# Identity products in place of transposes for step 0, masks on the tensor engine for three steps, three attention units to a bank, and 512-column transposes of x

## The chip, the cores and the metric

The kernel runs on one core of a Trainium2 chip. Times are device microseconds (us) of an execution; a kernel's time is the median over its runs. PE is the tensor engine (PEld its weight loads), DVE the vector engine, ACT the scalar engine, POOL the GpSimd engine, SP the sync engine. POOL and SP here only issue transfers (DMAs), apart from a few constants that POOL makes at the start.

## What is computed

Sliding-window attention with sink keys, and on its result a feed-forward layer with a rational activation:

```python
batch, n_heads, seq, head_dim = 4, 8, 768, 64
n_sink, window = 4, 128
scores = q @ k.T / sqrt(head_dim)
keep = (key < n_sink) | ((0 <= query - key) & (query - key < window))
a = softmax(where(keep, scores, -1e9))
x = (a @ v) laid out as (3072 tokens, 512)
h = x @ w_in                                  # 512 x 2048
P = a[0] + a[1]*h + a[2]*h**2 + a[3]*h**3
Q = 1 + abs(b[0])*abs(h) + abs(b[1])*h**2
out = (P / (Q + 1e-6)) @ w_out                # 2048 x 512
```

Inputs and the output are fp32; the products run in bf16 and accumulate in fp32.

## The kernel before

**Steps.** The 3072 tokens are cut into 12 steps of 256 (three to a batch entry). A step s has an attention part and then a feed-forward part, called m there.

*Attention.* Heads go in pairs, i = 0 to 3; two pairs make a group. k of a step is transposed and spread over `kT_fix` so that 64 keys of both heads of a pair fill one 128x128 weight (`spread_k`, L333 to L344). `scores` (L382) makes four products of 64 keys by 192 queries for a pair, into one tile of two PSUM banks; `exps` (L395, ACT) takes the exponential into `e_fix`; `mask` (L404, DVE) multiplies the two 64-column edge blocks of every 64 keys of a group by 0 and 1. Sink keys have products and exponentials of their own (L356, L366, and for the first step of a batch entry a small mask, L374). `attend` (L412) multiplies the exponentials of a pair with v, to which a column of ones is added for the softmax's sum: two tiles of 128 queries, 130 columns each, in one bank. `normalize` (L435) takes the reciprocal of the sums and multiplies, writing 256 columns of `x_n`. So a step has four attends and four normalizations, all on the bank `ps_m`, and each attend waits until the normalization before it has emptied that bank (in step 0 every second one uses `ps_o`). x is then transposed into `xblk`: in steps 0 to 2 on PE (`turn_x`, copied by ACT in `place_x`), from step 3 on by SP's transposing DMAs, four to a step, each 128 rows by 256 columns (`turn_x_tile`, L465).

*Feed-forward.* `project_in` (L475) makes 64 products of 256 columns in four blocks (called gemm1 in the plan), into the two-bank tiles `ps_h`, of which there are two; ACT copies each block into `hb`. DVE and ACT compute the activation in halves or whole tiles of 4096 columns: squares, |h|, denominator, polynomial, and 1/Q as exp(-ln Q) on ACT; `gate` is the last multiplication. The square of the first half is on ACT (step 0: DVE), that of the second half on DVE (L504; last step: ACT). `project_out` (L555) makes 2 x 16 products of 512 columns into `ps_o` (in the last four steps one of two into `ps_m`), ACT copies the result, SP stores it.

**The start.** q and k of step 0 come in by SP as fp32 (q as three tokens to a partition, k as two, so that the DMA has long runs), are cast by ACT (`cast_q3`) and DVE (`cast_k2`), transposed by PE, and put into order of tokens as they leave PSUM: `place_q3` (L275, ACT) writes bf16 with a stride of three, `spread_k2` (L312, DVE) with a stride of two, in eight copies. All other k, q, v and the weights come through POOL's cast DMAs. Those of steps 1 and 2 (`turn_k2`, `turn_q1`) are transposed by PE, later ones by SP's DMAs (L291, L307).

**Who sets the order.** The whole program is a list of pieces (`piece`, L586), each with its engine, an assumed length, a rank (a due time; four units are a step), the pieces it comes after, and the PSUM tile that it takes or frees. `run_list` (L842) plays these lengths forward: whenever an engine is free it takes the able piece of the lowest rank. The order that comes out is fixed in the program; each engine runs its list strictly in that order and waits where a piece's inputs are late on the chip. Where the plan leaves PE idle, `spin` (L351) is put in: products of the identity with itself that no one reads. POOL's and SP's DMAs are planned with an assumed load each, and at most eight of each kind are in flight.

## Time and profile before

| what | value |
|---|---|
| median of 11 runs | 276.99 us (273.23 to 280.5) |
| time of the profiled execution | 274.26 us |
| its span, first to last instruction | 272.5 us |
| PE busy, instructions | 245.9 us (90%), 2230 |
| DVE busy | 237.7 us (87%), 324 |
| ACT busy | 222.5 us (82%), 215 |
| POOL busy | 122.2 us (45%), 178 |
| software DMA queue (POOL) | 74288 packets, 12.99 MB, 77.5% of 16 engines' span |
| hardware DMA queue (SP) | 35936 packets, 14.73 MB, 28.4% |
| mean granted PE clock | 0.987 |

Busy time counts an instruction from its start to its end; a matmul's end is modelled, and neighbours overlap, so a PE that shows busy also holds the filler products of L353 (27.8 us in 334). Idle time in a row of a group is time that the engine stood just before it, with what ended the wait. In the chain of waits, which is followed back from the last instruction, each row is what the next one waited for. All engines run their lists in order, so a wait also holds up what stands behind it.

### The profile page before, as it was taken

To read this page: it belongs to the slowest core of one execution; us is meant where nothing else is said; L and a number is where in the kernel's file an instruction comes from. 1 tells how busy PE (TensorE), PEld (TensorE's weight loads), DVE (VectorE), ACT (ScalarE), POOL (GpSimd) and SP (SyncE) were. 2 spreads that over 40 slices of the span, in tenths; PEclk is the share of its full clock that TensorE was granted. 3 is DMA by queue.
4 is the path that set the end of the run, shared out by engine and by line. 5 is a ranking of instruction groups with operands and counts; after the bars stand their busy time and mean duration, and the time that the engine had idled before them with its cause. 6 is when DMAs were issued, how large, how long until landed. Compare 5 with 4: busy or idle time off the path is not lost.

```text
span 272.5 us, 5564 instructions
## 1 busy us (share of the span) xinstructions
PE 245.9 (90%) x2230; PEld 183.2 (67%) x2230; DVE 237.7 (87%) x324; ACT 222.5 (82%) x215; POOL 122.2 (45%) x178
## 2 busy tenths in 40 slices
PE   5768987998993799998999999998999999999895
PEld 5656976876861687786767757776676867665443
DVE  7774668999981899999999999999999999899960
ACT  8831787859996668999898989979989899799931
POOL 8945799789885776492951331560000000000000
PEclk9997999999999799999999999999999999999999
DMA  6999999999999999999999543381011111010132
GB/s 192 98 157 192 58 108 164 133 139 162 156 115 146 159 187 182 162 112 116 139 168 53 106 61 67 44 76 58 19 45 56 44 66 51 19 53 26 38 115 77
DMA packets 110249, 28.06 MB, mean 103 GB/s; under 512 B 102032, under 2 KB 106128, under 8 KB 110224
## 3 DMA queue, kind: packets, MB, share of 16 engines
q0 software_dynamic: 74288, 12.99, 77.5%
q1 hardware_dynamic: 35936, 14.73, 28.4%
q8 instruction: 17, 0.28, 0.4%
q14 instruction: 8, 0.07, 0.1%
HBM read 27.30 MB, written 6.29 MB: 123 GB/s over the span
## 4 chain that ended last, share of the span: by engine, by line
DVE 39%; DMA 15%; PE 14%; issue 11%; POOL 11%; ACT 9%; DVEq 0%; POOLq 0%
DVE den L515 6%; DVE sq L531 6%; PE ps_out L563 5%; DVE x_n L444 4%; PE ps_h L480 4%; POOL w_out_sb L184 3%; DMA q_bf<-in_q_dram 3%; POOL v_bd L175 3%; DVE num L521 3%; DVE sq L526 3%; DVE e L407 3%; DMA kT_flat<-k_bf 3%; DMA v_bd<-in_v_dram 3%; DVE sq L504 3%; DVE den L510 3%
## 5 line engine op out<-in xcount | busy, mean ns | idle before, releaser
L480 PE MATMUL ps_h<-xblk,w_in_sb 128*128 128x256 bf16 x768 | 92.3, 275 | 0.2
L563 PE MATMUL ps_out<-w_out_sb,g 128*128 128x512 bf16 x384 | 89.9, 379 | 1.3 <-ACT o_t L568 0.8
L175 POOL DMA_DIRECT2D v_bd<-in_v_dram x96 | 65.7, 704 | 39.4 <-PE ps_o L431 25.8
L480 PEld LDWEIGHTS <-w_in_sb 128*128 128x128 bf16 x768 | 74.6, 99 | 11.6 <-issue 0.8
L563 PEld LDWEIGHTS <-g 128*128 128x128 bf16 x384 | 36.8, 98 | 37.4 <-issue 1.3
L487 ACT ACTIVATE hb<-ps_h 128x1024 bf16<-128x1024 f32 x48 | 49.1, 1026 | 12.2 <-PE ps_h L480 12.2
L541 ACT ACTIVATE lnq<-den,one_eps,qsc 128x2048 f32<-128x2048 bf16 x24 | 50.3, 2098 | 9.5 <-DVE den L515 9.3
L400 ACT ACTIVATE e<-ps_s 128x768 bf16<-128x768 f32 x48 | 39.0, 818 | 9.2 <-PE ps_s L353 8.8
L547 ACT ACTIVATE den<-lnq 128x2048 bf16<-128x2048 f32 x24 | 46.1, 1923 | 0.0
L431 PE MATMUL ps_o<-v_bd,e 128*128 128x130 bf16 x352 | 30.2, 222 | 6.1 <-DVE e L407 4.0
L353 PE MATMUL ps_s<-ident 128*128 128x128 bf16 x334 | 27.8, 229 | 8.7 <-ACT e L400 7.3
L431 PEld LDWEIGHTS <-e 128*128 128x128 bf16 x352 | 24.5, 98 | 14.4 <-DVE e L407 5.0
L353 PEld LDWEIGHTS <-ident 128*128 128x128 bf16 x334 | 22.9, 103 | 10.4 <-issue 7.2
L515 DVE TENSOR_TENSOR den<-den,sq 128x2048 bf16<-128x2048 bf16 x24 | 29.2, 1218 | 0.1
L531 DVE TENSOR_TENSOR sq<-sq,hb 128x4096 bf16<-128x4096 bf16 (+1 forms) x13 | 27.6, 2124 | 0.3
L553 DVE TENSOR_TENSOR g<-num,den 128x4096 bf16<-128x4096 bf16 (+1 forms) x13 | 27.6, 2119 | 0.1
L535 DVE TENSOR_TENSOR num<-num,sq 128x4096 bf16<-128x4096 bf16 (+1 forms) x13 | 27.6, 2120 | 0.1
L151 POOL DMA_DIRECT2D q_bf<-in_q_dram x21 | 20.4, 985 | 11.2 <-DMA qT<-q_bf 11.2
L444 DVE SCALAR_TENSOR_TENSOR x_n<-ps_o,csc,rec 128x256 bf16<-128x256 f32 x48 | 23.2, 484 | 1.7
L390 PE MATMUL ps_s<-qT,kT 128*128 128x192 bf16 x192 | 23.9, 248 | 0.6 <-ACT qT L277 0.5
L502 ACT ACTIVATE sq<-hb 128x2048 bf16<-128x2048 bf16 x12 | 23.1, 1927 | 0.0
L167 POOL DMA_DIRECT2D k_bf<-in_k_dram x22 | 20.4, 940 | 2.6 <-DMA kT_flat<-k_bf 2.1
(76 smaller groups left out, 232.8 us busy)
## 6 DMA issues: line engine op xcount, KB each, us to landing
out_dram<-o_t SPq DMA_DIRECT2D x24, 256.0 KB, 2.2
v_bd<-in_v_dram POOLq DMA_DIRECT2D x96, 32.0 KB, 4.4
k_bf<-in_k_dram POOLq DMA_DIRECT2D x22, 128.0 KB, 5.7
q_bf<-in_q_dram POOLq DMA_DIRECT2D x21, 128.0 KB, 6.1
w_in_sb<-in_moe_w_in_dram POOLq DMA_DIRECT2D x8, 256.0 KB, 8.8
w_out_sb<-in_moe_w_out_dram POOLq DMA_DIRECT2D x16, 128.0 KB, 4.8
stage_q<-in_q_dram SPq DMA_DIRECT2D x1, 768.0 KB, 6.5
xblk<-x_n SPq DMA_TRANSPOSE x36, 2.7
```

What stands on the lines that cost most here:

```text
L175: nc.gpsimd.dma_start(out=v_bd[s][e * 64:(e + 1) * 64, i, :, e, 0:D], in_=v[b, h, g * TS:(g + 1) * TS, :].rearrange("(j p) d -> p j d", p=64))
L353: nc.tensor.matmul(ps_scores[:, 0, 384:384 + P], lhsT=ident, rhs=ident, start=True, stop=True)
L400: nc.scalar.activation(out=data.rearrange("p (a n) c -> p a n c", a=2), in_=ps[:, :, 0:384].rearrange("p a (n c) -> p a n c", n=2), func=A ...
L431: nc.tensor.matmul(ps_o[:, n, :], lhsT=l_, rhs=r_.rearrange("p e c -> p (e c)"), start=(m == 0), stop=(m == len(terms) - 1))
L444: nc.vector.scalar_tensor_tensor(out=dst, in0=o4[:, :, 0:D].rearrange("p (n e) c -> p n e c", e=2), scalar=csc, in1=rec.rearrange("p (n e) ...
L480: nc.tensor.matmul(ps[:, n, :], lhsT=w_in_sb[c][:, fc * P:(fc + 1) * P], rhs=xblk[m][:, c, :], start=(c == 0), stop=(c == NDMC - 1))
L487: nc.scalar.activation(out=hb[m][:, j * GW:(j + 1) * GW], in_=ps_h.pop((m, j)).rearrange("p n c -> p (n c)"), func=AF.Copy)
L515: nc.vector.tensor_tensor(out=den[m][:, c], in0=den[m][:, c], in1=sq[m][:, c], op=ALU.add)
L531: nc.vector.tensor_tensor(out=sq[m][:, c], in0=sq[m][:, c], in1=hb[m][:, c], op=ALU.mult)
L541: nc.scalar.activation(out=lnq[m, part], in_=den[m][:, c], func=AF.Ln, scale=qsc, bias=one_eps)
L547: nc.scalar.activation(out=den[m][:, c], in_=lnq[m, part], func=AF.Exp, scale=-1.0)
L563: nc.tensor.matmul(ps_out[m, tt], lhsT=g_of[m][:, co:co + P], rhs=w_out_sb[fc], start=(fc == 0), stop=(fc == NFFC - 1))
```

## The change

- **Order of step 0.** q and k of step 0 are no longer transposed in PE's transpose mode with a bf16 result. Each 128x128 block is the weight of a product with the identity, in fp32, and the result's columns are written to PSUM two or three apart, so that the tokens stand in order there. `place_q3` and `spread_k2` then copy runs; `spread_k2` has four copies instead of eight. The second half of q's cast moves from ACT to DVE. The tiles are `ps_s` and `ps_h` instead of `ps_o`, `ps_h` and `ps_m`.
- **Masks of steps 0 to 2.** Instead of DVE's `mask`, PE adds 0 or -1e9 to the edge blocks of the scores: two products of the identity with a 256-column tile after each pair's four. `mask_adds` makes the tiles; `mask_tiles` gets a later rank. The attends of these steps come directly after the exponentials.
- **Three units to a bank.** The eight (pair, query tile) units of a step are attended and normalized three, three and two at a time. `x_n` keeps its columns by unit.
- **512-column transposes.** A half of x (four units) is one transposing DMA of SP.
- **Ranks and engines.** PE's turning of k and q of step 1 gets a rank behind the first block of gemm1. The second half's square of steps 4 and 7 moves from DVE to ACT. The outputs of the last two steps take a `ps_h` tile for both query tiles. Some assumed lengths and loads of the plan are other numbers (among them w_in's load, 1.8 and 1.5 in place of 1.25).

The diff, cut to its core:

```diff
     def cast_q3(grp):
         h0, h1 = grp * H // 2, (grp + 1) * H // 2
-        nc.scalar.activation(
-            out=early[:, 0:NQ_HW, :].rearrange("p t (h d) -> p t h d", h=H)[:, :, h0:h1, :],
-            in_=raw["q"].rearrange("p (h t d) -> p t h d", h=H, t=NQ_HW)[:, :, h0:h1, :],
-            func=AF.Copy)
+        out = early[:, 0:NQ_HW, :].rearrange("p t (h d) -> p h t d", h=H)[:, h0:h1, :, :]
+        src = raw["q"].rearrange("p (h t d) -> p h t d", h=H, t=NQ_HW)[:, h0:h1, :, :]
+        if grp:
+            nc.vector.tensor_copy(out=out, in_=src)
+        else:
+            nc.scalar.activation(out=out, in_=src, func=AF.Copy)
...
+    def mask_adds():
+        nc.vector.tensor_scalar(out=edge_add, in0=edge, scalar1=-1.0, scalar2=1e9, op0=ALU.add,
+                                op1=ALU.mult)
+        nc.vector.tensor_copy(out=edge0_add,
+                              in_=edge_add.unsqueeze(1).to_broadcast([P, 2, 2, 64]))
+        for e in range(2):
+            nc.vector.memset(edge0_add[e * 64:e * 64 + NS, 0, 0, :], 0.0)
...
     def turn_q3(grp):

         if grp == 0:
-            ps = ps_op.tile([P, 512], FP32, tag="ps_out", name="ps_qT")
+            ps = ps_scores
         else:
-            ps = ps_hp.tile([P, 2, 512], FP32, tag="ps_h", name="ps_qT")[:, 0, :]
-        ps = ps.bitcast(BF16)[:, 0:2 * NQ_HW * P].rearrange("p (i t c) -> p i t c", i=2, t=NQ_HW)
+            ps = ps_hp.tile([P, 2, 512], FP32, tag="ps_h", name="ps_qT")
         for il in range(2):
+            dst = ps[:, il, 0:NQ_HW * P].rearrange("p (c t) -> p t c", t=NQ_HW)
             for t in range(NQ_HW):
                 c0 = (2 * grp + il) * P
-                nc.tensor.transpose(ps[:, il, t, :], early[:, t, c0:c0 + P], ident)
+                nc.tensor.matmul(dst[:, t, :], lhsT=early[:, t, c0:c0 + P], rhs=ident,
+                                 start=True, stop=True)
         ps_q["three", grp] = ps

     def place_q3(grp):
-        dst = qT_fix[0][:, 2 * grp:2 * grp + 2, 0:NQ_HW * P]
-        nc.scalar.activation(out=dst.rearrange("p i (c t) -> p i t c", t=NQ_HW),
-                             in_=ps_q["three", grp], func=AF.Copy)
+        nc.scalar.activation(out=qT_fix[0][:, 2 * grp:2 * grp + 2, 0:NQ_HW * P],
+                             in_=ps_q["three", grp][:, :, 0:NQ_HW * P], func=AF.Copy)
+    def turn_k0():
+        ps = ps_hp.tile([P, 2, 512], FP32, tag="ps_h", name="ps_kT0")
+        ps = ps.rearrange("p a c -> p (a c)").rearrange("p (i c t) -> p i t c", i=NPB, t=NTS)
+        for i in range(NPB):
+            for t in range(NTS):
+                nc.tensor.matmul(ps[:, i, t, :], lhsT=k_bf[0][:, t, i * P:(i + 1) * P], rhs=ident,
+                                 start=True, stop=True)
+        kT_flat[0] = ps.rearrange("p i t c -> p i c t")
...
-        src, kT = kT_flat[0], kT_fix[0]
         i0, i1 = 2 * grp, 2 * grp + 2
         for e in range(2):
             lo, hi = e * 64, (e + 1) * 64
-            for t in range(2):
-                nc.vector.tensor_copy(
-                    out=kT[lo:hi, :, lo:hi].rearrange(
-                        "p (i n) (c t) -> p i n c t", i=NPB, t=2)[:, i0:i1, :, :, t],
-                    in_=src[lo:hi, i0:i1, t, :].rearrange("p i (n c) -> p i n c", n=NHF))
+            nc.vector.tensor_copy(
+                out=kT_fix[0][lo:hi, i0 * NHF:i1 * NHF, lo:hi],
+                in_=kT_flat[0][lo:hi, i0:i1].rearrange("p i c t -> p i (c t)").rearrange(
+                    "p i (j c) -> p (i j) c", c=64))
...
+    def mask_on_pe(s):
+        return s < 3
...
             nc.tensor.matmul(ps[:, n // 2, (n % 2) * 192:(n % 2) * 192 + 192],
                              lhsT=kT_fix[s % 2][:, i * NHF + n, :],
-                             rhs=qT_fix[b % 2][:, i, c:c + 192], start=True, stop=True)
+                             rhs=qT_fix[b % 2][:, i, c:c + 192],
+                             start=(n % 2 == 0 or not mask_on_pe(s)), stop=not mask_on_pe(s))
+        for a in range(2 if mask_on_pe(s) else 0):
+            first_keys = g == 0 and a == 0
+            nc.tensor.matmul(
+                ps[:, a, :].rearrange("p (x c) -> p x c", c=64)[:, 0:6, :].rearrange(
+                    "p (n m) c -> p n m c", m=3)[:, :, 0:3:2, :], lhsT=ident,
+                rhs=edge0_add if first_keys else edge_add.unsqueeze(1).to_broadcast([P, 2, 2, 64]),
+                start=False, stop=True)
...
-    def attend(s, i):
+    UNITS = ((0, 3), (3, 6), (6, 8))
+    def attend(s, a):
...
-        grp, il = divmod(i, 2)
-        other = s == 0 and i % 2
+        u0, u1 = UNITS[a]
+        other = s == 0 and a == 1
         ps = (ps_op if other else ps_mp).tile([P, 512], FP32, tag="ps_out" if other else "ps_m",
                                               name="ps_o")
-        ps_o = ps[:, 0:NTS * 2 * (D + 1)].rearrange("p (n c) -> p n c", n=NTS)
-        for n in range(NTS):
+        ps_o = ps[:, 0:(u1 - u0) * 2 * (D + 1)].rearrange("p (u c) -> p u c", u=u1 - u0)
+        for u in range(u0, u1):
+            i, n = divmod(u, NTS)
+            grp, il = divmod(i, 2)
...
-        ps_a[s, i] = ps_o
-    def normalize(s, i):
-        ps_o = ps_a.pop((s, i))
-        if i == 0:
-            x_n[s] = a_x.tile([P, NTS, H * D], BF16, tag="x_n", name="x_n")
-        o4 = ps_o.rearrange("p n (e c) -> p (n e) c", e=2)
-        rec = a_x.tile([P, 2 * NTS, 1], FP32, tag="rec", name="rec")
+        ps_a[s, a] = ps_o
+    def normalize(s, a):
+        u0, u1 = UNITS[a]
+        ps_o = ps_a.pop((s, a))
+        if a == 0:
+            x_n[s] = a_x.tile([P, NTS * H * D], BF16, tag="x_n", name="x_n")
+        o4 = ps_o.rearrange("p u (e c) -> p (u e) c", e=2)
+        rec = a_x.tile([P, 6, 1], FP32, tag="rec", name="rec")[:, 0:2 * (u1 - u0), :]
         nc.vector.reciprocal(out=rec, in_=o4[:, :, D:D + 1])
-        dst = x_n[s][:, :, i * P:(i + 1) * P].rearrange("p n (e c) -> p n e c", e=2)

         nc.vector.scalar_tensor_tensor(
-            out=dst, in0=o4[:, :, 0:D].rearrange("p (n e) c -> p n e c", e=2), scalar=csc,
-            in1=rec.rearrange("p (n e) c -> p n e c", e=2).to_broadcast([P, NTS, 2, D]),
+            out=x_n[s][:, u0 * P:u1 * P].rearrange("p (u c) -> p u c", c=D),
+            in0=o4[:, :, 0:D], scalar=csc, in1=rec.to_broadcast([P, 2 * (u1 - u0), D]),
...
         ps = ps_hp.tile([P, GC, TS], FP32, tag="ps_h", name="ps_xT").rearrange("p n c -> p (n c)")
-        ps = ps.bitcast(BF16)[:, 0:2 * TS].rearrange("p (i c) -> p i c", i=2)
-        for il in range(2):
-            for n in range(NTS):
-                c0 = (2 * grp + il) * P
-                nc.tensor.transpose(ps[:, il, n * P:(n + 1) * P], x_n[s][:, n, c0:c0 + P], ident)
+        ps = ps.bitcast(BF16)[:, 0:2 * TS]
...
-            xblk[s] = xpool.tile([P, NDMC, TS], BF16, tag="xblk", name="xblk")
+        return xblk[s][:, 2 * grp:2 * grp + 2, :].rearrange("p i c -> p (i c)")
+    def place_x(s, grp):
+        nc.scalar.activation(out=x_half(s, grp), in_=ps_x.pop((s, grp)), func=AF.Copy)
...
+    def out_bank(m, tt):
+        if m >= NSTEP - 2:
+            return "ps_h"
+        return "ps_m" if m >= NSTEP - 4 and tt else "ps_o"
...
-                  lambda half=half, c=c: load_w_in(half, c), kind="sw", load=1.25)
+                  lambda half=half, c=c: load_w_in(half, c), kind="sw", load=1.8 if half == 0 else 1.5)
...
-    piece(("mask_tiles",), "DVE", 1.4, -17, mask_tiles, [("consts",)])
+    piece(("mask_adds",), "DVE", 0.5, -17, mask_adds, [("consts",)])
+    piece(("mask_tiles",), "DVE", 1.0, -7, mask_tiles, [("consts",)])
...
-        piece(("cast_q3", grp), "ACT", on_act(768), -21 + 0.1 * grp, lambda grp=grp: cast_q3(grp),
+        piece(("cast_q3", grp), "DVE" if grp else "ACT", 0.5 if grp else on_act(768), -21 + 0.1 * grp, lambda grp=grp: cast_q3(grp),
...
-              [("cast_q3", grp), ("consts",)], takes="ps_h" if grp else "ps_o")
-        piece(("place_q3", grp), "ACT", on_act(768, 0.2), -18 + 0.1 * grp, lambda grp=grp: place_q3(grp),
...
-        piece(("turn_q", n), "PE", 0.5, 4 * s - 17.5, lambda n=n: turn_q1(n),
+        piece(("turn_q", n), "PE", 0.5, 4 * s - 17.5 if s != 1 else -3.4, lambda n=n: turn_q1(n),
...
-            piece(("turned_k", s), "PE", 1.0, 4 * s - 18, lambda s=s: turn_k2(s),
+            piece(("turned_k", s), "PE", 1.0, 4 * s - 18 if s != 1 else -3.5,
+                  lambda s=s: turn_k2(s) if s else turn_k0(),
                   ([("load_k", s, t) for t in range(NTS)] if s else [("cast_k2",)])
-                  + [("consts",)], takes="ps_m")
+                  + [("consts",)], takes="ps_m" if s else "ps_h")
...
+        for a, (u0, u1) in enumerate(UNITS):
+            pairs = range(u0 // NTS, (u1 - 1) // NTS + 1)
+            grps = sorted({i // 2 for i in pairs})
+            r_ = NPB * s + (1, 2.5, 3)[a]
+            bank = "ps_o" if s == 0 and a == 1 else "ps_m"
+            piece(("attend", s, a), "PE", (u1 - u0) * (0.24 if g == 0 else 0.28), r_ - 5.2,
+                  lambda s=s, a=a: attend(s, a),
+                  ([("exps", s, i) for i in pairs] if mask_on_pe(s) else
+                   [("mask", s, grp) for grp in grps]) + [("spread_vs", b)]
+                  + [("load_v", s, h) for h in range(2 * pairs[0], 2 * pairs[-1] + 2)]
+                  + [("sink_mask" if g == 0 else "sink_exps", s)], takes=bank)
+            piece(("norm", s, a), "DVE", 0.355 + (u1 - u0) * 0.133, r_ - 5.1,
+                  lambda s=s, a=a: normalize(s, a),
+                  [("attend", s, a), ("scalars",),
+                   ("turned_x", s - 2) if s >= 2 and a == 0 else None], frees=bank)
...
-            piece(("mask", s, grp), "DVE", 0.6, NPB * s + 2 * grp + 1 - 7 - 0.05,
+            if not mask_on_pe(s):
+              piece(("mask", s, grp), "DVE", 0.6, NPB * s + 2 * grp + 1 - 7 - 0.05,
...
-            norms = [("norm", s, 2 * grp), ("norm", s, 2 * grp + 1)]
+            norms = [("norm", s, grp), ("norm", s, grp + 1)]
...
-                for n in range(NTS):
-                    piece(("turn_x", s, grp, n), "SP", 1.25, r_,
-                          lambda s=s, grp=grp, n=n: turn_x_tile(s, grp, n), norms + [free],
-                          kind="hw", load=0.6)
-                piece(("placed_x", s, grp), "NONE", 0.0, 0, None,
-                      [("turn_x", s, grp, n) for n in range(NTS)])
+                piece(("placed_x", s, grp), "SP", 1.25, r_, lambda s=s, grp=grp: turn_x_half(s, grp),
+                      norms + [free], kind="hw", load=0.8)
...
+    SQ_ACT = (4, 7, NSTEP - 1)
...
-        if m < NSTEP - 1:
+        if m not in SQ_ACT:
```

## The prediction

> **What bounds the kernel now.** I read the busy table by stage first (cut where the chain of waits changes character), then the chain of waits, then the groups by line and shape, then the order in time of each engine.
>
> ```profile
> core 0: us, PE busy (x) PEld busy (x) DVE busy (x) ACT busy (x) POOL busy (x), PEclk, DMA share, GB/s
> 0.00:22.50 22.50, 14.77 (x189) 12.71 (x190) 16.29 (x55) 14.58 (x24) 17.02 (x38) 0.99 1.16 153
> 22.50:48.40 25.90, 22.33 (x269) 19.66 (x267) 17.73 (x30) 17.06 (x19) 21.57 (x31) 0.94 1.62 127
> 48.40:80.00 31.60, 30.30 (x304) 24.71 (x304) 31.23 (x39) 26.24 (x26) 27.51 (x39) 1.00 1.93 143
> 80.00:90.00 10.00, 5.03 (x38) 2.76 (x36) 3.36 (x8) 6.20 (x5) 5.79 (x8) 1.00 2.41 138
> 107.00:160.00 53.00, 50.54 (x465) 37.88 (x463) 52.37 (x68) 50.15 (x46) 28.01 (x36) 1.00 1.38 120
> 160.00:232.00 72.00, 70.24 (x604) 51.36 (x603) 70.62 (x85) 66.77 (x61) 10.27 (x16) 1.00 0.28 53
> ```
>
> Up to 48.4 us every engine has slack. From 48.4 to 80 and from 107 to 160 DVE is 99% busy. From 160 to 232 PE is full as well: per step its order in time has 4 blocks of L480 at 1.75 us, 4 of L563 at 1.73, 4 attends at 0.57, 4 scores at 0.33 and 0.44 for the sinks, 17.9 us, and the steps recur every 17.9 us (L521 at 188.66 and 206.62). Between 80 and 90 nearly everything stands. The chain of waits says why, and why the start is late:
>
> ```profile
> 12.78 9.31 DMA q_bf<-in_q_dram
> 22.14 0.61 PE ps_qT L285 x4
> 22.75 4.90 PE ps_h L480 x32
> ...
> 72.09 6.65 DMA k_bf<-in_k_dram
> 78.75 8.48 DMA kT_flat<-k_bf
> 87.33 0.51 DVE kT L341
> ```
>
> x of step 0 is ready at 19.57 (second copy into xblk), but PE, in order, has the turns of k and q of step 1 ahead of the first product and waits for their loads until 22.14. The first 32 products then take 4.90 us instead of 3.5, at a lower clock. In the middle DVE waits 6.6 us for k of step 5, issued by POOL only at 71.2.
>
> ```profile
> L407 DVE TENSOR_TENSOR e<-e,edge 128x1024 bf16<-128x1024 bf16 x24 | 16.4, 683 | 1.8 <-ACT e L400 1.8
> L444 DVE SCALAR_TENSOR_TENSOR x_n<-ps_o,csc,rec 128x256 bf16<-128x256 f32 x48 | 23.2, 484 | 1.7
> L341 DVE COPY kT<-kT_flat 64x1024 bf16<-64x1024 bf16 x18 | 8.8, 486 | 6.7 <-DMA kT_flat<-k_bf 6.6
> L341 DVE COPY kT<-ps_kT 64x1024 bf16<-64x1024 bf16 x4 | 2.8, 689 | 3.7 <-PE ps_kT L304 3.7
> L319 DVE COPY kT<-ps_kT 64x256 bf16<-64x256 bf16 x8 | 3.1, 438 | 0.1
> L277 ACT ACTIVATE qT<-ps_qT 128x768 bf16<-128x768 bf16 x2 | 2.7, 1455 | 0.0
> L400 ACT ACTIVATE e<-ps_s 128x768 bf16<-128x768 f32 x48 | 39.0, 818 | 9.2 <-PE ps_s L353 8.8
> ```
>
> Behind the bar stand the busy us, the mean ns of one, and the idle time before it. These means are the prices below. "In a row" is the distance of starts in the order in time, shorter than the duration.
>
> **What the Trainium skill says.** "VectorE: DVE Perf Modes", Why PSUM operands drop a tier: a PSUM source is held to two elements a cycle, fp32 to one. The trace agrees for bf16: L341 takes 689 ns from PSUM and 486 from SBUF. So 64x512 fp32 costs the cycles of 64x1024 bf16: 689 ns alone, about 0.61 in a row (an estimate from this section and L341's row). "TensorE: Matmul & The Clock Gate", What's actually happening: PE's clock is gated down after an idle window and comes back only after sustained work. The trace agrees: PEclk 0.83 in 20 to 30 and in 90 to 100 us, each after a PE pause. "DMA: Bandwidth & Descriptors", Issuing engines are not separate DMA queues: SP's and POOL's transfers share 16 engines. The trace agrees: a 256-column x transpose lands in 2.7 us (median) but in 6.6 when issued at 72.85, beside POOL's loads.
>
> **The change, part by part** (against the profiled execution: span 272.5, its time 274.26; both lie below the median 276.99, so I subtract the sum from the median).
>
> *Step 0.* Placing q: 2 x 1455 ns become two contiguous copies at 818, 0.69 in a row: ACT is free at about 10.8 instead of 12.1. Spreading k: 8 x 0.39 = 3.1 us become 4 x 0.61 = 2.4. One q cast (836 ns on ACT) goes to DVE at about 0.5 (L159 casts 1024 columns in 0.63). The 20 identity products replace 20 transposes at 0.057 each; output columns 12 bytes apart appear in no row, so between 0 and double, +1.1 us; I take 0[...]. Both masks, 0.68 us and a wait each, leave the chain; 4 exps at 0.69 after 10.8 end at 13.8, the last attend and norm take 1.3, turn and copy 1.1: x ready at about 16.3, 3.3 us sooner. mask_tiles (1.0 us) moves behind, under ACT's exps (10.8 to 13.5); without that cover it costs its 1.0, for sink_mask needs it. mask_adds costs about 0.6 on DVE, under the turning of k.
>
> *First product.* The turns of step 1 (8+8 transposes, no DMA) go behind its first block on PE; their DVE copies, 1.8 us, follow. What is late next is w_in: POOL's own waits show its half 0 landed one chunk after the other until 19.8 (the load at 19.82 waits for it). So it starts at 19.9 instead of 22.54, and warm: 2.6 + 1.3 = 3.9 us. The next gate stays: w_in half 1 lands at 29.4, when POOL's last wait on it ends and PE starts its third block. Scores of step 1 (28.49) can start at about 24.5, so this ACT work fills the slack before 29.4. POOL's order, k and q of step 2 (landing near 36) and of step 5 do not move. Of 3.9 I count 3.0, as PE and DVE work that then stands ahead of the stall at 80.5.
>
> *Masks of steps 0 to 2.* Six L407 leave DVE (4.1 us); of the four of steps 1 and 2 (32.96, 39.69, 46.39, 55.21) only the last lies in its full stage, 0.6. PE gets 24 products of 256 columns at 0.109 (an L480 product) = 2.6 us; their repeated operand and gapped output are in no row, so up to double, 5.2. Both fit under the 18.6 us that PE spends on L353, its filler products, before 66; without that cover they cost 2.6 to 5.2. Each pair lies between scores and exp, +0.22 in the loop over the one scores bank, where ACT in steps 1 and 2 has other copies to do. I count 0.6.
>
> *Three units per bank.* Per step, 4 x (484 + 176 of its reciprocal L441) = 2.64 us become 2 x (617 + 176) + 660 = 2.25. The 384-column norm is in no row: between 484 and 726 (in proportion); I take 484 + 128 x 1.04 = 617, one fp32 column a cycle from PSUM as the section above has it. Of 0.39 x 12 I count where DVE is full, 2 steps before 80 and 3 from 107 to 160: 1.9. From 160 to 232 PE bounds; there one of four returns of the bank goes, and PE's waits of its sink products for x_n were 1.5 in three places: 0.7. The middle unit needs both masks, so x's first half comes later and its second as before; the second sets the start of the product. Sum 2.6.
>
> *Squares of steps 4 and 7 to ACT.* DVE -1.22 each, ACT +1.93. Step 4's lies in 107 to 160, where ACT has only 2.85 us idle: 0.8 of 1.22. Step 7's lies under a full PE: 0.4. Sum 1.2.
>
> *512-column x transposes.* SP issues 18 instead of 36, 1.2 us each. A half was issue 1.2 + landing 2.7 = 3.9; the new one is not in the trace. The q and k transposes of that shape land in 2.4 to 8.0 (medians 5.3 and 6.3), all before 155 us. Between -1.5 and +2.4 a step; I take 0, since late steps have a free DMA.
>
> *Tail.* Outputs of the last two steps take ps_h. PE's wait of 0.8 on the output copy (253.98) and some of 1.2 us of gaps after it go: 1.0. The other planned lengths (w_in 1.8 and 1.5) only reorder; priced in the rivals.
>
> Sum: 3.0 + 0.6 + 2.6 + 1.2 + 1.0 = 8.4. Span 264.1, own time 265.9 (274.26 - 8.4), median 268.6 (276.99 - 8.4).
>
> **Rivals.** (a) The front gain dies at the stall: kT of step 5 still lands at 87.3 and PE, in order, only waits longer. For it: POOL is full from 30 to 78. Left are 1.8 (norms after 107) + 1.2 + 1.0 = 4.0: 273.0. (b) The opposite: x of step 3 comes early enough for its four product blocks (7.0 us) to fill the hole at 80.5 to 87.3, of which PE lost 5.3. Against it: its scores wait for q until 61. 5.5 more (the 5.3, and some of the slow clock after it): 263.1. (c) Slower: the 512-column transpose lands late. x of step 11 had its last piece issued at 231.8, landing about 234.5; its product starts at 235.39. The new one, issued at 230.5, decides from a landing of 4.9 us up; at 6.3 it costs 1.4 a step, 9 steps, 12.6: 281.2. For it: those medians. Against: DMA share 0.28 after 160. (d) The change does nothing: ACT (93 to 95% busy from 107 on) takes over what DVE gives: 277.0.
>
> **How the numbers follow.** Forecast 0.38 (own range 265.5 to 272), (a) 0.22, (b) 0.20, (c) 0.12, (d) 0.08. The range 261.5 to 277.5 leaves out about 0.07 of (b) below and most of (c) with the upper edge of (d), 0.13, above. One per cent, 2.8 us, is about what a measurement tells from no change. Faster: 0.37 + 0.15 + 0.20 = 0.72; within: 0.01 + 0.07 + 0.07 + 0.03 = 0.18; slower: 0.09 + 0.01 = 0.10.
>
> **What would show it.** First L480 near 19.9, third block still near 29.4; L444 at 618 ns for 384 columns, 36 in all; six L407 fewer; DVE about 10.8 us less busy (4.1 + 4.7 + 2.4 + 0.7 - 0.5 - 0.6); the xblk landing below 4.9 late. Wrong if the wait at 87 grows past 10 us, if PE waits for xblk each step, or if step 0's x comes after 19.8.

## The result, and the profile after

| | before | after |
|---|---|---|
| median of the runs | 277.27 us (273.11 to 280.7, 47 runs) | 272.98 us (270.89 to 274.51, 12 runs) |
| profiled execution, its span | 274.26, 272.5 us | 272.19, 270.5 us |
| PE, DVE, ACT busy | 245.9, 237.7, 222.5 us | 250.3, 230.2, 224.2 us |

The medians lie 4.3 us apart; the ratio is 0.9901, 95% interval [0.9867, 0.9934]. It leaves out executions more than 1.5% above the fastest of their kernel, and since before's executions scatter widely it drops more of before, and lies closer to 1 than the ratio of the medians (0.985). So the change is worth 1.0 to 1.5%, where I had forecast 3% (8.4 us). The time is that of rival (a), but not by its mechanism: the stall at 87 did not stay.

First the busy table of the changed kernel, cut as before's was (for each engine busy us and instructions, then the granted PE clock). Behind it stands the one row of before that has not been shown yet.

```profile
core 0: us, PE busy (x) PEld busy (x) DVE busy (x) ACT busy (x) POOL busy (x), PEclk, DMA share, GB/s
22.50:48.40 25.90, 21.87 (x306) 20.13 (x304) 17.34 (x23) 15.83 (x17) 19.81 (x28) 1.00 1.20 106
48.40:80.00 31.60, 28.14 (x276) 22.39 (x276) 26.88 (x32) 25.63 (x26) 26.64 (x37) 1.00 1.94 154
80.00:90.00 10.00, 10.00 (x97) 7.51 (x95) 6.71 (x12) 9.34 (x11) 8.24 (x12) 1.00 2.11 150
90.00:107.00 17.00, 14.42 (x115) 10.83 (x114) 13.51 (x15) 11.28 (x11) 12.70 (x17) 0.90 1.85 178
107.00:160.00 53.00, 50.82 (x495) 39.66 (x492) 50.96 (x61) 49.93 (x46) 27.61 (x35) 1.00 1.38 123
160.00:232.00 72.00, 71.87 (x622) 53.20 (x621) 69.72 (x77) 70.65 (x65) 10.46 (x16) 1.00 0.27 52
```

```profile
90.00:107.00 17.00, 15.97 (x146) 12.91 (x144) 15.65 (x21) 13.09 (x13) 12.04 (x16) 0.90 2.23 178
```

The hole of 80 to 90 is closed: PE 10.00 instead of 5.03. But the stages beside it got emptier: 48 to 80 has DVE at 26.88 instead of 31.23, and 90 to 107 has PE at 14.42 instead of 15.97, with the mean clock at 0.90 in both kernels. The gate (L589, L553 before; the last DVE operation of a step) of step 2 ends at 107.4, at 107.6 before: until there the two kernels are level. The gain comes after it: the last gate ends at 261.0 instead of 263.6.

The chain of waits says what the new delays are:

```profile
10.55 8.45 DMA w_in_sb<-in_moe_w_in_dram
19.29 9.77 DMA w_in_sb<-in_moe_w_in_dram
...
31.70 6.34 DMA q_bf<-in_q_dram
...
92.10 5.59 DMA xblk<-x_n
97.73 8.60 PE ps_h L516 x62
```

Both halves of w_in, then q of step 2, and then x of step 3 instead of kT of step 5. The first of these are the known gates: the first product starts at 19.55, its third block at 29.10. The second shows in PE's order in time (start, length, line; in brackets the idle time before it):

```profile
34.00 0.39 PE L468 MATMUL ps_o<-v_bd,e 128*128 128x130 bf16 x4
...
38.08 0.40 PE L310 MATMUL ps_qT<-ident,q_bf 128*128 128x128 bf16 x4 [2.00 <-DMA q_bf<-in_q_dram]
...
39.49 0.39 PE L468 MATMUL ps_o<-v_bd,e 128*128 128x130 bf16 x4
...
46.73 0.39 PE L468 MATMUL ps_o<-v_bd,e 128*128 128x130 bf16 x4
...
51.27 0.93 PE L516 MATMUL ps_h<-xblk,w_in_sb 128*128 128x256 bf16 x7
```

The three units of step 1 start at 33.4, 39.5 and 46.7. The second stands in order behind the turn of q of step 2; the third finds the one ps_m bank taken by the sink scores of step 2, whose exp comes behind a logarithm on ACT. So the product of step 1 starts at 51.27, where it started at 48.4 before. And SP's queue, in order:

```profile
84.04 1.28 SPq L504 DMA_TRANSPOSE xblk<-x_n  x1
85.41 2.83 SPq L335 DMA_TRANSPOSE kT_flat<-k_bf  x2
88.34 3.67 SPq L318 DMA_TRANSPOSE qT<-q_bf  x2
92.10 1.22 SPq L504 DMA_TRANSPOSE xblk<-x_n  x1
```

x of step 3 is normalized at 84.1, but its second half is issued only at 92.1, behind four transposes of k and q. PE stands from 95.2 to 97.7.

The groups by line and shape confirm several of the prices that I had worked out:

```profile
L481 DVE SCALAR_TENSOR_TENSOR x_n<-ps_o,csc,rec 128x384 bf16<-128x384 f32 x24 | 14.8, 618 | 0.8
L439 DVE TENSOR_TENSOR e<-e,edge 128x1024 bf16<-128x1024 bf16 x18 | 12.3, 682 | 0.8 <-ACT e L432 0.8
L342 DVE CAST kT<-ps_kT 64x512 bf16<-64x512 f32 x4 | 2.8, 689 | 0.3 <-PE ps_kT L301 0.3
L293 ACT ACTIVATE qT<-ps_qT 128x768 bf16<-128x768 f32 x1 | 0.8, 804 | 0.0
```

617 ns was forecast for 384 columns, six masks fewer, 689 and 818 ns for the copies. These prices were right; what they buy was not. DVE is 7.5 us less busy (237.7 to 230.2), not 10.8.

### The profile page after: what moved, and what is told of

Same layout as the page of the kernel before. It is cut to its first block, busy times and chain, and to the rows that moved or that the text cites. A ratio compares the mean times of both kernels' runs of the same rounds, so it can differ in the third digit from the quotient of the medians.

```text
span 270.5 us, 5670 instructions
## 1 busy us (share of the span) xinstructions
PE 250.3 (93%) x2315; PEld 190.7 (70%) x2315; DVE 230.2 (85%) x293; ACT 224.2 (83%) x216; POOL 122.9 (45%) x178
## 4 chain that ended last, share of the span: by engine, by line
PE 50%; DMA 20%; ACT 8%; POOL 7%; DVE 7%; issue 3%; SPq 3%; ACTq 0%; POOLq 0%
PE ps_out L613 22%; PE ps_h L516 19%; DMA w_in_sb<-in_moe_w_in_dram 7%; PE ps_o L468 4%; DMA q_bf<-in_q_dram 4%; DMA qT<-q_bf 3%; POOL w_out_sb L188 3%; PE ps_s L414 2%; POOL v_bd L179 2%; DMA xblk<-x_n 2%; DMA v_bd<-in_v_dram 2%; DMA w_out_sb<-in_moe_w_out_dram 2%; PE ps_s L373 2%; POOL k_bf L171 2%; ACT lnq L577 1%
## 5 line engine op out<-in xcount | busy, mean ns | idle before, releaser
L179 POOL DMA_DIRECT2D v_bd<-in_v_dram x96 | 63.7, 684 | 43.3 <-PE ps_o L468 29.6
L523 ACT ACTIVATE hb<-ps_h 128x1024 bf16<-128x1024 f32 x48 | 49.7, 1043 | 12.5 <-PE ps_h L516 12.2
L432 ACT ACTIVATE e<-ps_s 128x768 bf16<-128x768 f32 x48 | 39.8, 834 | 7.5 <-PE ps_s L420 4.2
L373 PE MATMUL ps_s<-ident 128*128 128x128 bf16 x395 | 30.8, 229 | 6.9 <-ACT e L432 5.2
L373 PEld LDWEIGHTS <-ident 128*128 128x128 bf16 x395 | 26.6, 104 | 8.5 <-issue 5.9
L468 PE MATMUL ps_o<-v_bd,e 128*128 128x130 bf16 x352 | 28.5, 219 | 0.1
L589 DVE TENSOR_TENSOR g<-num,den 128x4096 bf16<-128x4096 bf16 (+1 forms) x13 | 27.6, 2122 | 0.6 <-ACT den L583 0.5
L538 ACT ACTIVATE sq<-hb 128x2048 bf16<-128x2048 bf16 x14 | 27.1, 1937 | 0.1
L171 POOL DMA_DIRECT2D k_bf<-in_k_dram x22 | 21.7, 993 | 6.4 <-DMA kT_flat<-k_bf 5.4
L618 ACT ACTIVATE o_t<-ps_out 128x512 f32<-128x512 f32 x24 | 14.6, 615 | 10.5 <-PE ps_out L613 8.1
```

Of the source, the lines that this page charges most:

```text
L179: nc.gpsimd.dma_start(out=v_bd[s][e * 64:(e + 1) * 64, i, :, e, 0:D], in_=v[b, h, g * TS:(g + 1) * TS, :].rearrange("(j p) d -> p j d", p=64))
L373: nc.tensor.matmul(ps_scores[:, 0, 384:384 + P], lhsT=ident, rhs=ident, start=True, stop=True)
L432: nc.scalar.activation(out=data.rearrange("p (a n) c -> p a n c", a=2), in_=ps[:, :, 0:384].rearrange("p a (n c) -> p a n c", n=2), func=A ...
L468: nc.tensor.matmul(ps_o[:, u - u0, :], lhsT=l_, rhs=r_.rearrange("p e c -> p (e c)"), start=(m == 0), stop=(m == len(terms) - 1))
L523: nc.scalar.activation(out=hb[m][:, j * GW:(j + 1) * GW], in_=ps_h.pop((m, j)).rearrange("p n c -> p (n c)"), func=AF.Copy)
```

## The experiments

Two kinds. "Old order": the plan is drawn with the pieces of before, and each piece then does new work, so that little else moves. (Where the units of three are in it, the exponentials of a step's second pair also go behind the third attend of the step before; f_front moves the turns of step 1 as well.) "Own order": the changed kernel, with one part taken back or one move made in its finished order. d is the difference of the medians of all executions, kernel minus before, both measured together on one chip; its 95% interval comes from resampling them. The ratio is formed as in the result above. Where the two disagree, the text says so. Comparisons with after_again are of two such differences, and for a_front2, a_x, a_sqdve, a_tail and a_both these were not measured together.

| run | d, us | ratio |
|---|---|---|
| f_all, old order | +2.7 [1.0, 4.1] | 1.0225 [1.014, 1.031] |
| f_front, old order | -0.4 [-1.7, 0.4] | 1.0109 [1.0048, 1.0171] |
| f_units, old order | -3.6 [-6.0, -1.8] | 0.9922 [0.9846, 0.9998] |
| f_x512, old order | -3.4 [-4.6, -1.8] | 0.9971 [0.9931, 1.0011] |
| f_tailsq, old order | +4.1 [1.4, 5.7] | 1.0145 [1.0091, 1.02] |
| f_tail, old order | +0.8 [-1.0, 2.5] | none given |
| r_const | -0.7 [-3.6, 1.6] | none given |
| b_k5 | -3.2 [-3.9, -2.5] | 0.997 [0.9938, 1.0002] |
| b_spin | -2.7 [-3.3, -1.7] | 0.9974 [0.9937, 1.0011] |
| fu_k5 | -6.4 [-7.0, -5.5] | 0.987 [0.9835, 0.9904] |
| after_again | -4.2 [-5.0, -3.4] | 0.991 [0.9872, 0.9947] |
| a_front2, own order | -6.3 [-7.2, -4.2] | 0.9765 [0.9735, 0.9795] |
| a_sqdve, own order | -1.5 [-2.3, -0.3] | 1.0045 [0.9997, 1.0093] |
| a_norm4, own order | -2.8 [-3.5, -1.8] | 1.0034 [0.9971, 1.0098] |
| a_tail, own order | -5.0 [-6.5, -4.0] | 0.9809 [0.9763, 0.9855] |
| a_spin, own order | -4.9 [-5.4, -3.8] | 0.9856 [0.9822, 0.9889] |
| a_x, own order | -3.4 [-4.2, -1.6] | 0.9891 [0.9849, 0.9933] |
| a_both, own order | -5.5 [-7.5, -1.8] | 0.9774 [0.9719, 0.9829] |

**All parts, the front, the units, and the planner's numbers.** My theory: the parts are worth their price, and the redrawn order takes some of it back. The rival: the order is everything.

```
f_all    each piece of the old plan does the new work (units of 2, 3, 3
         blocks in the places of pairs 0, 2, 3; both halves of x in the
         place of the second)
f_front  step 0 and the masks so, and
+    late_ = [("turned_k", 1), ("turn_q", 3), ("turn_q", 4), ("spread_k", 1), ...]
+    todo[n_:n_] = moved_          # behind ("gemm1", 0, 1)
f_units  units and 512-column transposes so
r_const  -kind="sw", load=1.25
         +kind="sw", load=1.8 if half == 0 else 1.5     (and 1.72, 1.73, +0)
```

> The parts of the change set into the order of the kernel before: the plan is drawn with the old pieces, and each piece then does the new work (masks of steps 0 to 2 on PE, three units to a bank, 512-column transposes, products for step 0, squares of steps 4 and 7 on ACT, the last two steps' outputs in ps_h). The turns of step 1 stay ahead of the first product, so the 3.0 us of the front are not in it. Theory 1 (the parts are worth about what I priced, and the redrawn order takes some of it back): 8.4 - 3.0 = 5.4 us off, about 272. Theory 2 (the redrawn order is the whole gain, since it takes away the stall at 80 to 87, and the parts are worth nothing): 276.5 to 277.5, with the stall still at 87. Theory 3 (ACT becomes the bound where the squares went): 276 or more, with DVE idle behind ACT in 107 to 160.

> Step 0 alone in the old order: identity products, masks of steps 0 to 2 on PE, and the turns of k and q of step 1 moved behind the second block of the first product. The prediction has 3.0 + 0.6 us for this: 273.4. Theory 1 (the w_in gate at 29.1 and the loads of step 2 take the earlier start away): within 0.8 of before, 276.2 to 277.5, first L480 product near 20, third block still near 29.

> Three units to a bank and 512-column transposes of x alone, in the old order (units of 2, 3 and 3 blocks in the places of the first, third and fourth pair; the first half of x goes with the second). The prediction has 2.6 + 0 us: 274.4. If units are worth nothing because PE and ACT bound by then: 277. If the later first half of x costs: over 278, with PE waiting for xblk in each step.

> The kernel before with only the planner's numbers of the change (a w_in chunk 1.8 and 1.5 instead of 1.25, product blocks 1.72 and 1.73, no extra on the hidden copies): no work is changed, only the order. Theory 1 (a redrawn order moves the time by some us either way, by luck): 274 to 281, a new set of waits. Theory 2 (these numbers are the gain): 273, and the stall at 87 gone.

f_all fell outside both theories: slower by either measure, by 2.7 us or 2.3%. Some part costs time when the order does not fit it; nearly the same work in its own order (after_again) is 6.9 us faster (2.7 + 4.2). f_front settles my largest term: its first product starts at 18.6 (22.5 before), but kT of step 5 is spread at 87.0, as late as before (87.3), and nothing is left at the end: 0.4 us by the medians, within the scatter, and by the ratio 1.1% slower. The old order thus does to the front what rival (a) said. r_const draws another order by the same rules and shows no gain, so a redrawn order need not gain by itself; its six executions leave room for a gain of up to 3.6 us. f_units gains 3.6 us by the medians and 0.8%, about 2 us, by the ratio, where I had 2.6; but it does not gain where I had it: from the first product of step 4 to that of step 11 it takes 120.5 us against 121.3. What it gains stands ahead of that, at the stall: the first product of step 3 starts at 94.6 instead of 98.45, and kT of step 5 is spread at 85.1.

**What of the units, and which part costs.**

```
f_x512   -                    lambda s=s, grp=grp, n=n: turn_x_tile(s, grp, n)
         +   nothing at n = 0, one 512-column half at n = 1; norms as before
b_k5     +    n_ = [w.name for w in todo].index(("load_v", 4, 0))
         +    todo[n_:n_] = early_          # both ("load_k", 5, t)
fu_k5    f_units and b_k5
f_tailsq -square(m, B_, "dve")
         +square(m, B_, "act" if m in (4, 7) else "dve")   and out_bank
f_tail   out_bank alone
```

> Only the 512-column transposes of x, in the old order and with the old units of 256 columns: SP issues one instruction for a half of x where it issued two, the first place of each pair stays empty. The prediction has 0 for this (276.8). If what the units' run gained came from SP's queue (k of step 5 transposed earlier, because fewer x transposes stand ahead of it): 273 to 275, with kT of step 5 spread near 85 instead of 87.3. If it came from the norms on DVE: 276.5 to 277.5.

> The kernel before with one move: POOL issues the two loads of k of step 5 ahead of the eight v loads of step 4. If the stall at 80 to 87 and the low PE clock behind it are what the change took away, this alone gives most of its gain: 273 to 274.5, kT of step 5 spread at 83 to 85 (SP's queue then decides), and a narrower spread of runs. If the gain comes from the parts: 276.5 or more.

> Three units and 512-column transposes in the old order, and the loads of k of step 5 ahead of the v loads of step 4. If both work on the same stall, the gains do not add: 271.5 to 273. If they add (3.6 and 3): 270.

> Only the squares of steps 4 and 7 on ACT and the outputs of the last two steps in ps_h, in the old order. The prediction has 1.2 + 1.0 us: 274.6. Since all parts together in the old order were 2.7 us slower than before, and step 0 and units alone were not: 278 to 280 here, with DVE waiting for ACT's square of step 4 and of step 7.

> The kernel before with only the outputs of its last two steps in ps_h, in the old order. The prediction has 1.0 us for this: 1.0 below before. If the tail in that order is what costs (the first product of the last step then finds no free ps_h bank): 1 us above before, and the squares the rest of the 4.1.

By the medians f_x512 alone has what f_units has: the part that I priced at 0. Its kT of step 5 is spread at 85.6. b_k5, two loads moved on POOL's queue, has as much (85.1). By the ratio each of the two is within 0.3% of before, so what they take away is mostly the slower part of before's scatter; the part on the pauses says what that part is. f_units and b_k5 together (fu_k5) are faster by either measure, and their gains add: in each alone DVE still waits 3.7 and 3.8 us for kT of step 5, in fu_k5 it no longer does. f_tailsq finds the costly part. These are two of its waits between 107 and 232; before has neither (us in all, times, longest):

```profile
DVE rec L441 <- PE ps_o L431: 2.6, 3, 1.2
DVE den L515 <- ACT sq L502: 2.5, 2, 2.3
```

A square that leaves a full DVE for ACT comes back here as a wait of DVE where ACT's turn comes late. With f_tail at +0.8, the squares are by difference the other 3.3 us, with an interval of 0.5 to 5.4.

**The changed kernel in its own order.**

```
a_front2 +    todo = put([("exps", 1, 3), ("attend", 1, 1), ("norm", 1, 1), ("turn_x", 1, 0),
         +                ("attend", 1, 2), ("norm", 1, 2), ("exp", 0, 0), ("placed_x", 1, 0),
         +                ("turn_x", 1, 1), ("placed_x", 1, 1)], ("turned_k", 2))
         +    todo = put([("gemm1", 1, 0)], ("scores", 2, 1))
         +    todo = put([("gemm1", 1, 1)], ("attend", 2, 0))
a_x      +  ("placed_x", s, 1) on SP directly behind ("norm", s, 2), s from 3
a_both   both
a_sqdve  -square(m, B_, "act")
         +square(m, B_, "act" if m > 7 else "dve")
a_norm4  +        cuts = (0, 4, 6) if a == 0 else (0, 2 * (u1 - u0))
         +   one reciprocal and one norm for each cut
a_tail   -            bank = out_bank(m, tt)
         +            bank = "ps_m" if m >= NSTEP - 4 and tt else "ps_o"
```

> The changed kernel with its own order, except between 33 and 51 us: the second and third unit of step 1, their norms and the two turns and copies of x of step 1 go ahead of the turns of k and q of step 2 (and ahead of the logarithm on ACT), and the first two blocks of the product of step 1 go ahead of the later scores of step 2. If the front's gain was lost there (PE standing in order for q of step 2 until 38.1, one ps_m bank, ACT's order), the product of step 1 starts near 43 instead of 51.3, and the time falls by 2 to 4 us, to 269 to 271 where the changed kernel gives 273. If the earlier start only meets the next gates: no change, within 1 us.

> The changed kernel with one rule added to its order: on SP's queue the second half of x of each step from 3 on is issued as soon as its last norm is done, ahead of the k and q transposes that stood before it. If x of step 3, normalized at 84.1 and landed at 97.7, was held up by SP's queue and that wait (2.5 us on PE) counts: 270 to 271.5. If kT of step 6 then comes later by as much: 272.5 to 273.5.

> The reordered front of a_front2 and the earlier x on SP's queue of a_x together. If SP's queue is the next gate once step 1 comes earlier: 1 to 2 us below a_front2, that is 7.3 to 8.3 below before. If not (a_x alone gave nothing): 6 to 6.5 below before, as a_front2 alone.

> The changed kernel in its own order with the second halves of the squares of steps 4 and 7 back on DVE. The prediction has 1.2 us for having them on ACT: 274.2 here. If ACT had become the bound in the changed kernel (rival d of the prediction): 272 or less. In the old order the squares and the tail together cost 4.1 us; if that came from the place in ACT's order and the redrawn order fits them: 274 to 275 here.

> The changed kernel once more, as the measure for the runs beside it on this chip: 1 to 1.5% below before, as at first.

> The changed kernel with the first unit's norm in two pieces of 256 and 128 columns, each with its own reciprocal: about 0.34 us more of DVE per step (0.401 + 0.21 from the trace in a row, and an estimate of 0.26 + 0.2 for 128 columns, less 0.534 + 0.223), which is what three units save. If the norms' price counts where DVE is full (seven to nine steps): 2 to 3 us above the changed kernel. If PE or the copies bound there: within 0.7.

> The changed kernel in its own order with the outputs of its last two steps back in the ps_o and ps_m banks. If ps_h is worth the 1.0 us of the prediction: 1.0 above the changed kernel (3.2 below before instead of 4.2). If the tail is bound by DVE's and ACT's chain to the last gates anyway: within 0.5 of it.

a_front2 is 2.1 us below the changed kernel (6.3 - 4.2, interval -0.1 to 3.4) and by ratio 1.5%: much of the front's gain was lost in the order between 33 and 51. Its product of step 1 starts at 47.5, less early than I expected (43), since filler products stand before it in PE's order and wait there for ACT. Its PE pause at step 3 is 1.4 us, and the clock stays at 1.00. The clock alone does not explain the gain: the profiled execution of after_again has no low clock there either, and its gate of step 2 ends at 107.0, that of a_front2 at 103.7.

a_x brings nothing, and a_both no more than a_front2: SP's queue is no gate by itself. a_sqdve loses 2.7 us (4.2 - 1.5, interval 1.6 to 4.0) and 1.4% by the ratio, so in an order that was drawn for them the squares are worth twice my 1.2. a_norm4, measured together with after_again, loses 1.35 us [0.6, 2.5] by the medians and 1.2% by the ratio: by the medians the fewer norms are worth about half of my 2.6. (It gives back the fourth norm of a step, not the fourth return of the bank.) a_tail, instead of losing 1.0, lies 0.8 below, which is within its interval: the outputs in ps_h are not seen to help. In the traces the time from the last gate to the end is 8.9 us before and 8.5 in a_tail, and 9.5 after and 10.0 in f_tail, the two with ps_h.

**The pauses of PE.** In both kernels a PE pause is followed by a low clock. These are slices of 1.5 us, of before and then of the changed kernel:

```profile
85.50:87.00 1.50, 0.00 (x0) 0.00 (x0) 0.00 (x0) 0.83 (x1) 0.61 (x1) 1.00 1.70 142
87.00:88.50 1.50, 0.00 (x0) 0.00 (x0) 1.13 (x3) 0.00 (x0) 1.32 (x2) 1.00 2.14 132
...
90.00:91.50 1.50, 0.60 (x8) 0.48 (x6) 1.47 (x4) 1.23 (x2) 1.50 (x3) 0.62 2.95 174
91.50:93.00 1.50, 1.50 (x17) 1.50 (x15) 0.98 (x1) 0.56 (x2) 0.97 (x2) 0.50 2.33 136
```

```profile
96.00:97.50 1.50, 0.00 (x0) 0.00 (x0) 1.46 (x3) 0.43 (x1) 1.50 (x2) 1.00 2.09 207
...
99.00:100.50 1.50, 1.50 (x9) 1.04 (x8) 1.50 (x3) 0.53 (x2) 1.50 (x3) 0.50 1.74 195
100.50:102.00 1.50, 1.50 (x10) 1.08 (x9) 1.50 (x1) 0.92 (x1) 1.50 (x4) 0.59 1.96 177
102.00:103.50 1.50, 1.50 (x16) 1.34 (x15) 1.47 (x2) 0.63 (x1) 1.01 (x2) 1.00 1.74 250
```

PE stands for 3.8 us (before) or 2.5 us, runs again, and is then granted half the clock: in the changed kernel 9 or 10 matmuls in a slice instead of 16. Two runs fill the pause and change nothing else.

```
b_spin   +        if w.name == ("attend", 4, 0):
         +            spin(56)
a_spin   +        if w.name == ("gemm1", 3, 0):
         +            spin(42)
```

> The kernel before with 56 filler products (3.2 us) on PE ahead of the first attend of step 4, where PE stands from 85.3 to 89.0; the landing of kT of step 5 is left at 87.3. If the low clock behind the pause is a cost of its own: no slice below 1.00 between 88 and 96, and 1.5 to 3 us less than before, with a narrower scatter. If only the landing counts: within 0.7 of before.

> The changed kernel with 42 filler products (2.4 us) ahead of the first product of step 3, where PE stands from 95.2 to 97.7. If the low clock behind that pause (0.50 for about 4 us, so 2 us of work) is what the new wait costs beside itself: 1 to 2.5 us below the changed kernel. If DVE sets the pace from there on: within 0.7 of it.

The same time in b_spin:

```profile
85.50:87.00 1.50, 1.50 (x8) 0.68 (x7) 0.00 (x0) 1.50 (x3) 0.35 (x1) 1.00 2.05 155
87.00:88.50 1.50, 1.50 (x28) 1.44 (x26) 0.00 (x0) 1.26 (x1) 1.23 (x2) 1.00 1.77 180
...
91.50:93.00 1.50, 0.74 (x14) 0.74 (x14) 1.46 (x4) 1.20 (x2) 1.48 (x2) 1.00 2.54 158
```

DVE still waits, so the landing is not better, but the clock stays full, and the median falls by 2.7 us. The scatter narrows from 270.2 to 279.1 down to 271.5 to 276.0; by the ratio the gain is not distinguishable from none. So the pause costs its low clock in many executions of before, not in the best ones. The mean granted clock of every execution bears this out. One stretch of 3.4 us at half clock takes 0.006 off it. Of the 199 executions of before that were measured beside these runs, the 30 above 0.99, with one such stretch or none, have a median of 271.7 us, and the 77 below 0.983, with three or more, one of 277.1. Above 0.99 are 6 of the 65 executions of before beside b_spin and 19 of the 22 of b_spin, and 17 of the 66 beside b_k5 and f_x512, 20 of the 22 of b_k5 and 16 of the 22 of f_x512. In the changed kernel filling the new pause gives 0.75 us [-0.3, 1.3] below after_again by the medians, and 0.5% by the ratio: little, if anything. DVE is busy through that pause (1.46 of 1.50 us at 96.0), which may be why.

## Why the prediction was wrong

**First product at 19.9, warm, third block still at 29.4:** right (19.55, 29.10, clock 1.00). x of step 0 was ready at 18.5, not 16.3, still ahead of the gate. The identity products cost not 0.057 but 0.109 each (the upper end of my range), and the eight of k twice that in the profiled execution, as the last section shows.

**"Of 3.9 I count 3.0": this step failed.** I took the earlier front as work that stands ahead of the next stall, and did not follow it through the next in-order waits. In place of 3.0 us f_front gives 0.4, not distinguishable from nothing. In the change the order of step 1 gives the front's lead back: the first product starts 3.0 us sooner than before, that of step 1 2.9 us later (51.3 instead of 48.4). a_front2 shows that another order keeps about 2 us.

**"POOL's order, k and q of step 2 and of step 5 do not move": wrong.** Changed lengths redraw the whole plan. POOL issues k of step 5 at 66.3 instead of 71.2 and kT of step 5 is spread at 80.6 instead of 87.3, so the stall that I held fixed went, and with it, by b_spin and b_k5, about 3 us of the median. In exchange came the waits for q of step 2 and for x of step 3. I had set aside the other planned lengths as what "only reorder", and did not price the low clock behind the stall, though the profile before shows 0.90 there.

**512-column transposes, taken as 0:** in the old order 3.4 us by the medians, 0.3% and uncertain by the ratio. In the changed kernel the landing takes 2.4 us after 160, far below the 4.9 of rival (c); before 160 its median is 5.1 us, but PE waits for it only once. What the old order gains with them is not shorter waiting in SP's queue: in before and in f_x512 SP stands ready for the k transposes of step 5 and waits for POOL's load of k, and issues the second of them at 78.75 and at 78.55. It is the landing that is shorter: kT is spread 8.6 us after that issue in before and 7.0 in f_x512. One x transpose is in flight beside it in before (issued at 72.85, landed at 79.46) and none in f_x512; that this is the reason is not shown.

**Three units, 2.6:** 1.35 [0.6, 2.5] for the fewer norms in its own order. One error is a price: I summed durations, but in a row a 256-column norm and its reciprocal take 0.401 + 0.210 us and the longer ones 0.534 + 0.223, so a step saves 4 x 0.611 - 2 x 0.757 - 0.611 = 0.32 and not 0.39.

**Squares, 1.2:** the sign was right in its own order (2.7) and wrong in the old one (a cost of 3.3). **Tail, 1.0:** not seen; 0.8 the other way in both orders, each within its interval. **Masks:** prices right (0.22 us a pair); not tried alone.

So the 4.2 us of after_again are, taken back one at a time, mostly squares (2.7) and norms (1.35), less the tail, and about 1 for the rest, in which the stall that went and the two waits that came are not separated. Such parts need not add. The front's 3.0 is not among them. Rival (a) had the time by leaving out the front; it thought that the stall would eat it, which is so in the old order, while in the new one the stall went and the order of step 1 took its place. That its sum came so near is luck: the norms came out smaller than it had them, the squares larger, and the tail did not show. Rival (d), that ACT takes over, is out: ACT is 98% busy from 160 to 232, yet giving work back to DVE loses time.

fu_k5 (268.49) and a_front2 (269.37), each on its own chip, beat both kernels, 6.4 and 6.3 us below before. f_all suggests that fu_k5 would not gain by taking the other parts in the old order. The two were not joined. Left open: what the masks are worth alone, what the new order is worth with the old work, why kT lands earlier in f_x512 and whether that makes up the whole of its 3.4 us, and the 512-column transposes in the changed kernel's own order.

## What to carry to other kernels

Where a planner writes the order, price a change twice: its operations in the old order, and the order it causes; a part that fits one order (squares on ACT) can cost three microseconds in the other. An earlier start is worth only what passes every in-order wait behind it, so follow it to the next gate before counting it. Where PE stands, count the clock after the pause too, and try filler products before anything larger.

## What the runs showed of the hardware

**Strided output columns.** Products that write fp32 PSUM columns 8 or 12 bytes apart run at half pace. In f_front, whose clock is full there (the filler L372 goes at 0.056 each):

```profile
6.40 1.05 PE L300 MATMUL ps_kT<-ident,early 128*128 128x128 bf16 x8 [1.90 <-DVE early L163]
7.24 1.66 PE L372 MATMUL ps_s<-ident 128*128 128x128 bf16 x26
8.73 0.82 PE L287 MATMUL ps_s<-ident,early 128*128 128x128 bf16 x6
```

From start to start such a product takes 0.109 us, k's and q's alike, and the filler, which writes the same type side by side, 0.056. The filler loads the same weight each time while each identity product brings a new one, but that is not the reason: the transposes of the same blocks in before go at 0.056 each, and so do the products of `attend`, each with a new weight and fp32 columns side by side. A gap between blocks of 64 columns, as the masks have it, costs nothing that shows: 0.22 us for two products of 256 columns.

In the profiled execution of the changed kernel the products of k go at 0.213 and the filler behind them at 0.107, until 9.57 us, and then at 0.056: half the clock for 3 us. The profile's clock column reads 1.00 there, but this trace's first clock record starts only at 9.57, so the 1.00 ahead of it is no reading. In after_again, whose records start at 4.17, the same products take 0.109, and x of step 0 is ready at 17.95 instead of 18.5.

**Pause and clock.** The length of a pause does not decide. One of 2.5 us in the changed kernel was followed by half clock, one of 3.2 us in after_again, at the same place, was not, nor one of 1.4 us in a_front2. The Trainium skill ("TensorE: Matmul & The Clock Gate", What's actually happening) has the clock judged over free-running windows of about 3.4 us, and low after an idle one. The clock records agree on the windows: in all 20 profiled executions the low stretches last 3.41 us, or two or three times that (but for the last, at the program's end), and each starts a whole number of 3.41 us after the first record. Where the pause falls between these marks decides. In the changed kernel it lies within one window (94.90 to 98.31), in which PE is busy for 0.89 us, and the half clock begins at 98.31. In after_again it is divided between two (92.92 to 96.33 and 96.33 to 99.74), in which PE is busy for 1.66 and 1.97 us. On idleness the traces differ from the page: a window need not be idle. At full clock, every window in which PE was busy for less than 0.44 of the time was followed by half clock (17 of them), and of those above 0.49 only one (0.56, in f_tail); in between both happened.

**Issue and landing of a transpose.** SP takes 1.2 us to issue a transpose of x, whether of 256 columns (before) or of 512 (after), and after 160 us, beside little other traffic, they land in medians of 2.3 and 2.4 us. So a half of x in one transpose costs SP half the time that it does in two.
